# Feed-forward gate and u in transposed layout, heads loaded four at once, and a new order table, in a sparse-attention and gated-MLP kernel

## The chip, the cores and the metric

The kernel runs on one core of a Trainium2 chip. The metric is the device time of one execution in microseconds (us), the median of several. Traces are from the hardware profiler. Engines are named as in the profile: PE (TensorE matmul), PEld (its weight loads), DVE (VectorE), ACT (ScalarE), POOL (GpSimd), SP (SyncE, which here only issues DMAs).

## What is computed

For 4 batches of 8 heads, 768 positions and head size 64: every query attends to the 6 best of the 24 key chunks of 32 positions, chosen by an upper bound from each chunk's minimum and maximum of k; then a gated feed-forward (spatial gating unit) runs on the joined heads.

```python
# attention, per batch and head (q, k, v: 768 x 64)
k_min, k_max = min and max of k over each chunk of 32
ub  = sum(maximum(q * k_min, q * k_max))        # 768 x 24, causal
top = the 6 largest chunks of each row
attn = softmax(q k^T / 8 where chunk in top and causal)
x   = attn v                                     # heads joined: 768 x 512 per batch
# feed-forward, per batch
h = relu(x @ w_in); u, v = h[:, :512], h[:, 512:]
v_n = (v - mean) / sqrt(var + 1e-6)
v_s = w_spatial @ v_n + b_spatial[:, None]       # mixes positions
out = (u * v_s) @ w_out
```

## The kernel before

**Work units.** Heads are worked in 16 pairs (two heads that are neighbours). A head's 768 positions are 6 tiles of 128. Each pair goes through `load_ops`, `prep_ops` (`prep_first` for the first) and `attend_ops`; after every fourth pair a batch is complete and `mlp_ops` runs for it.

**Loading.** `load_ops` issues, on POOL's queue, one DMA for k of both heads (`kp`), two for q (`qs`, one for each head) and one for v (`vt`); the DMA also casts f32 to f16. For the first pair a head's k or q may instead go through SP into an f32 tile `stage` and be cast by an engine.

**Preparing a pair.** k is transposed into `kT`, either by PE (6 matmuls with the identity, then a copy out of PSUM on DVE or ACT) or by a transposing DMA on SP's queue. The chunk extremes are six DVE instructions: two of `t1` (16 against 16), two of `t2` (8 against 8), two reductions into `kmm` (lines L477, L480, L483); for the first pair one head at a time (L580, L584, L588). Small copies spread them into `km` and copy `kT` into `kh` (helper lines L243 for ACT, L245 for POOL, L249 for DVE). q is transposed by PE (L505), evacuated as `rq`, multiplied with `km` (the bounds, L517), and `max8` and `select` write the chunk choice into `qs`, which is transposed into `a` (PE, L553, or SP's DMA).

**Attention.** Scores come out on PE in six groups of columns for each head (L672), ACT makes the exponentials `e` out of PSUM (L683), the causal triangle is put on either by an extra PE matmul (L675), POOL (L694) or DVE (L692), and 21 matmuls of 65 columns multiply with v (L703). DVE normalises into `x16` (L713, L717), which PE (L734) or a DMA (L727) transposes into `xT`.

**Feed-forward of a batch.** For each of 6 position tiles: `v` = 4 matmuls of 512 columns (L752), relu into `vraw`, statistics (L758, L760), and DVE's `vn` (L769). `u` = 4 matmuls of 512 columns with `xT` as weights (L779), relu into `u`. The spatial product: 6 matmuls of 512 columns with `wsT` as weights (L793); then one DVE instruction makes `g = (product + bias column) * u` (L797). `g` has positions on partitions, so it is transposed into `gT`: on SP's queue (L801) or by PE (L807) with a copy. The output product is 4 matmuls of 512 columns (L814), a copy `o`, and a store from SP's queue (L819).

**The order.** Nothing of the order on an engine is left to a scheduler. Every operation is first entered in a list with the engines that could do it and their costs. The string `PLAN` is then run through: each three characters are one operation, the first two its number (in base 64) and the third its engine and PSUM bank. Operations that have two forms (PE or DMA for a transpose, PE or POOL/DVE for the triangle) stand in the list twice, and the table names one of them. So each engine's queue, SP's and POOL's among them, is the table's order, and an instruction that waits holds up all that stand behind it on its engine.

```python
for c in range(0, len(plan), 3):
    hi, lo, how = (DIGITS.index(x) for x in plan[c:c + 3])
    o = self.ops[64 * hi + lo]
    ...
    if o.take is not None:
        o.take.tile = self.banks[how // 4 - 1]
    if len(o.alts) > 1:
        o.emit(list(o.alts)[how % 4])
```

Of the kernel before, what the change touches and what calls it, by code (L numbers as in the profile page):

```python
# [8 lines left out]
F32 = mybir.dt.float32  # L9
F16 = mybir.dt.float16  # L10
# [4 lines left out]
P = 128  # L15
# [22 lines left out]
def blocks(half):  # L38
# [13 lines left out]
    "0k00000140F00900500600K00O00V00l10Q00J00q00X00280R10U00C00wC0N00A003G0m00G00800T10r10M00W01FK0B0"  # L52
    "2N00s00H00I007016O0S13h02RS0x00z00y00/00+01311511102P01001411G01H02O01Q11I01J01711K01L03i004W121"
    "1M04/02S01O10P01R43j01N11802U00v01981S01A02V02e21P11B01T12W00YG1C01UC1V02h25002f23lK2g21DW0Z02X0"
    "0D03m12Y05101W02Z01E12iS1X02k053O2j01Y42d23p00f01r82a22c21Z03r01oG2b22lK2Q05413z18L02m040C2DW1lS"
    "3+124O1t05703o08N02748M00e01q04112n01y83q01n02901/G2o03t01+03s02102AS2sK5K43w05603v12C02q81iG3u0"
    "2t05804202602F05L03US3W01k03RK3x05M03GO5900g03y143C1aW9f04402r04503T03/10E01c01dS4603J423G3X83L0"
    "1f039K9h03Z05A02H02I02xW8P45B02z033S3B05I15E25C08Q05D23I05F24AC3O85J14B048W1hK1v08g49g03Q08S05NC"
    "4901w08i05G13508h14iO4k05204CW5O02J03k05P01x00a04E05H14a84c02K04QS8U02u42w05Q04FG8T03NO4H03b03c0"
    "8V03d08W0Az04NW4oK4d84P06PC3049jG8X08b036W6Q05UO8Z08Y08a04f04l83205S45V04KCCH09k00L04q00c03804TK"  # L60
    "4n08e15T08f16JO9m04V09n04rW6K04t04M09+G5u88jK5Z42/W3D08k05xC5WOA008c14S05b08l05w09/05kS0d05Y04J4"
    "5z04X05m063866O60G9o04Y08m06505eC9y18d15g04Z03E08qS9w16204hK6988o46B09p09q09r08r04v03F08p09u25nC"
    "5hGB189t00b09v2B206809s05p04w04x0B505j05/S3fWA+09TOA/0FR09Q49R0A1C3g15d8A209U06D08tG4z49x1A30CI0"
    "5r05s0A4092K8u077W4+09z18/O930900CLG98C6LK6R49NO6E0990A50Gl05t06F09i0CM06M19F89WCCJ06HS6fKB709G0"
    "6VGB406I09X0B90BF2B609I8B80CO06pC0h0BH29J06W0CP0BE1BIS7809O06X0BK1BA0790BG0BB06q06S0958BJ07GOCQ0"
    "8wG6T4CR06g06Y0BC0CT0FVSBD0BLW8x06aG6U1Ca19Y1FS06r0BM0FW09607H07I06b0B006c0BN08O06z46h0AkCAl0CS0"
    "CX0Aq87DS6Z0FT0AMOCZ1AN09A06+0BO06/0AZGAa06s0CcKAEW6i0CY16d06j0CV06uCAF0FZ0CU0CW16e06v06w09K0AhO"
    "An46k0Cd0BP0Ce06l0AJG6t0Ar00i0Ao07AW700I30AK07MC7N07O06x0Ai0CfK6N8Cb1Cg0710AS46O06y07206n0Ch08y0"
    "7E06m0Ci07JGFY0ABCAs0AP87F0AcOAd07K0Fk1AQ07B07309LS9Z0740Gr08zOFm8Cj0Ae07C0AT0Gn06o07L09B0JN0AC0"
    "C8K750Fl17ZW9C0760BV4BdGAU0Fj17a07jCC90BW0Be0Fi1BgKBh0Af47b0I90Fa0Fb0Fc0At0BmG9a0AG0Fd0BYKFf07k0"  # L70
    "9b07l0Fn19D0C2SAu0Bn0Fo1Fe2BjOBtG7P8Fg0Fh07c07m0Bu0FpW7Q0C30C5CGm0Av0Gs0B/4I50Fq0Bk0C60BZ0BwGBx0"
    "81S820C00DPOI40JP07R0DMCDSKDT0Gt0DQ0Fr0Fs0DEWFt0Bo0Gv0AHGAV0Cs47S0IA0H017U8CK0AW0AX0Gu07d0DN0By0"
    "DJK7V0DK0DU0IC0CA0Ba0Ct0IE08309c0Nr0Aw08BOD4GD50H4C7o87p0Gw0H61IB0ID0Go0840C+KCp4Cq08C0IF0DBGC/0"
    "DC0DF0DG07t88D0Bb47u0D1KD20Gx0G+2Bp0CxSCy0BzGG/2Gz1H11IJ0D60CB0Bq0GOWH50H21Br07v0CC0G8KG90CD0GWC"
    "Gy1GP08E0FzS7W47w0DHGH32DV0Cu0CE0F+0G5KDW0DX0GLWJROH78GX0JS0CvSIH0GTCJO0D70H80GZG7X0JV0GM0GU0II0"
    "H90G60Gc4Jh17Y0Gd0IOOIG1G0WHA07gCIP1DbKIQ07q4IR8MX0G10D80D90JX07h0DZOIS0JZ0Ga0HB0GBWGESDgCGe1GC0"
    "Da0JU0FU0MZ0IT0GF0E3G850Jf1NvWJe2Jg1Dc08F0IL17r0Dh0DlODm0E40IU0JW0Dd1De0IK2Di0Dn0JY0Do0Dj0Dk0D+S"
    "D/0E01Dv4GG0ED8Nw1P90IV0E10Jc0Jb2HtCE50HVKHW0HSOHqWEE0Hu0EF1IM1Jd2HYGJa0HZ0E20Hr0EJS7x0JiKHHCHI0"
    "Dw0Nz0N/0Dp0Df0Dx0GQ0Ny0Jk0Jj1EGGHf8IN1Dq0EH0HwWN+0EI0E60Dy0Dr0E70GRCGf0ES4Du0HT0Md0EPKEQ0Ns0ER1"
    "JQ0ET0Hg0EK0Hx0Gg0EU1Dz0E80G207i0JlGJm0MY0EL0HnOJ08J10G3KGH0HKWDs0884HL0Jn0Jo0EMSGI0Ho0E90Dt0Iz8"  # L80
    "HiWHj0EA0Jp0Gh0Hk0I60Me0Mg0EN0Mf0IbGEB0EO0HPOHQ0Mh0EC07s0Nt0GJ0Ic07+W7/0EpSJ5CEq0Ha1Mj0Mo1IjOHy0"
    "J8G890EVWEW0Mp1EX08I4J90I+0IpGMsKIe8Mi0Er0Ik0Mk0Mm1Gi0Mr2HlOIq0EY0Mn2O10EZ0J60If0Mq1Ml0QU0KHWEfG"
    "Eg0Mt0PDCEs0O00HM0Is8PE0Mu1Eh0JBS8J0PB0MvKIt0Ez4PA0O30JC0Hz0JECIg0O52Ei0Mw0HN8Hb0JF0Mx0KKGMy0E+0"
    "KYSKI0KL0ImCOAKO41E/0H+0H/0Ej0KZ0FHWFI0QT0OB0PG0FJ0Mz0Hc0QV0OC1F00JvGIn0Iu1PI0O20F7SPH0KVOO71O82"
    "Jw0Hd0KSKODCOE0KT0O91K74PJ0800K80JG0F80F90KW0KAGEt0FK0KP88K0FA0O61IhKOF0KQ0KM0PU4QZ0J20PS1K4WJ3O"
    "Ka0JH0JI0KB0JySPW1K50K18KNGJz0J+0K20OG0JJ0KC0Kb0PL0Iv0EmCNfWIw0NZONHSKc0Ec8Ix0NUKNg0NI0N3WJ/SPK0"
    "PV0KD08A0Kd0NE4PO1KE0KF0QoGPN2Ed1Qq0Na0I00NV0N6OEwKN40NiWNF0PM0En1NcSN70Ex0Qp0Kf4PP0NKOPX8LVKNj0"
    "Kg1L4WKrCNd0NRGQb0JK0PT2PY0PZ0NB4KmSKs0Kn0NS0Qd0L50LW0N80OH0Pa0Qa0Qc0Qe0Qf0ONGP08NL0Kt0NC0F10OYO"
    "Ma0OeCKo0L94Nu0Qj1Ku0LA0P10LX1Nk0Pb0Of0KhSOQ8L60Ki0Kv0Qg0OzCLSKLPWLQ0Kj1OZ0LB1Qh0ObOQl0OR0Qi2PQ1"
    "Kk0OO0Oc0OV8O+0OtSLR1QrGNW0Kp0Qs0Kq0LT0NX4Nl0OS0N9OEe0Ou0LYCOwWOW0FL0Q3SLU0LZ0Ox0PR1Ph8Nm0Pi0Qm1"  # L90
    "Qt0Qu0Nn0NM0NN0Qk1Q40PyKK/WQ6GQ70FB0LC0Kl0La1Eo0Kw0QE8QF0L00Kx0L11L20L30F44F50Pz0OoSOp0PpGP21OlC"
    "Pq0QB8QC0Om0NO0L70L80LD0NP0FOWQH4Q81LMKQI0LJSPC0LE0PvGKy0Kz0QW0LN0LO1LK0Qv0QK8QL0Og0LF0PkOLL0Pl0"
    "Ey0FECOT4Q/8Oh0LlKLG0Oq0OrSLH0P30LI0FP0Oi0Pw0K+0Oj0Pm0R00RGOLvWRH0LbGMN8P40P50PsOLm0Lc0Pt0R74QM1"
    "R80Ln0Ld0FF0P+0Lo0Lw0Q9SLe0Qn1RbORQ4RVKRW0Rc0RR0QN0RNCPnGP/0MDKRO0RDOQO0QP0P60No0R2SME0R30Lf0Re4"
    "Q00R41RACQ10Lp0Lx0RE0QQ0RS0RYSMO0RB0Ly0Rf0MP0RI0MF0SYORTGRZ0R5CF60RJ0Rg0Rh0FQ0RK0M34RL0Ri0Rj0MG0"
    "M40M50RnWRlSMQ0M60RxCRsGS5KRm1Rt0Ry0SP8Rz0R+0Ru1Rv0R/0SASRw0SF4Ro0SG0SH0SI0Rp0Rq0S60SQ0SB0M70Lz0"
    "MH0S70SJ0LsCRr0SC0S00S80S10MR0LiGSV4S30S90SD0SW0Lj0SSWS40ST0MAKSZ0FG0SE0M0SS20SK0SL0SM0Sa1SX0S/G"
    "SR0SN0SO0SU1T94Lk0M11Lt0Lu0TA0MB0T00MC0Sh8Si0Sj0M20T10Sk0T20SrOSs0St0Sl0MKCTB0Su0TJKTK0SwWML0TC0"
    "T30MUSMM0Sb8SoGSc0T6OSx1MV1TD0Sd1SyCSp0TT4TL0SeWSz1Sf0TU0TV0TM0MW0TOSTGGSq0T70Sg1TW0TP1T80TH0TY8"
    "TQOS+0TR0TI0TS0TZ0TaCTb0Tc0"  # L100
# [95 lines left out]
def kernel(  # L196
# [35 lines left out]
    G_XBAR = 3  # L232
# [41 lines left out]
    bcol = cp.tile([P, NQT], F32, name="bcol")  # L274
    braw = cp.tile([NQT, P], F32, name="braw")
    idf = cp.tile([NQT, NQT], F32, name="idf")
# [4 lines left out]
    ws_raw = cp.tile([P, NQT, S], F16, name="ws_raw")  # L281

    kp_r = ring(3, [P, 2, NQT, D], F16, "kp")
    qs_r = ring(4, [P, NQT, 2, P], F16, "qs")
    v_r = ring(4, [P, 2, NQT, D + 2], F16, "vt")
    stage_r = ring(4, [P, NQT, D], F32, "stage")
    kT_r = ring(2, [P, S], F16, "kT")
    kh_r = ring(3, [P, 2, S], F16, "kh")
    t1_r = ring(2, [P, 2, NCH, CHUNK // 2], F16, "t1")
    t2_r = ring(2, [P, 2, NCH, CHUNK // 4], F16, "t2")  # L290
    kmm_r = ring(2, [P, 2, NCH], F16, "kmm")
# [14 lines left out]
    u_r = ring(12, [P, DH], F16, "u")  # L306
    g_r = ring(4, [P, DH], F16, "g")
    gT_r = ring(6, [P, KO, P], F16, "gT")
# [21 lines left out]
    def const_ops():  # L330
# [23 lines left out]
        for j in range(len(qs_r)):  # L354
            s.op(("DVE", 0.4, 0.45), lambda j=j: preset(qs_r[j]), -98 + j,
                 w=[("sel", j)])
            s.op(("DVE", 0.1, 0.2), lambda j=j: nc.vector.memset(v_r[j][:, :, :, D:D + 2], 1.0), -97 + j,
                 w=[("ones", j)])
# [6 lines left out]
        for j in range(len(kh_r)):  # L365
            for hi in range(2):
                s.op([("ACT", 0.72, 0.87), ("DVE", 0.45, 0.58)], lambda e, j=j, hi=hi: copy(
                    e, kh_r[j][D * hi:D * hi + D, hi, :], ex, False), -40 + 10 * j, r=["ex"], w=[("exrow", j, hi)])
        s.op(("SP", 0.45, 0), lambda: nc.sync.dma_start(out=braw, in_=moe_b_spatial.rearrange("(t p) -> t p", p=P)),
             -60, w=["braw"], load=0.1, tag="lb")  # L370
        s.op(("DVE", 0.06, 0.16), lambda: nc.vector.tensor_copy(idf, identity[0:NQT, 0:NQT]), 19, r=["identity"], w=["idf"])
        bb = Bank("tr")
        s.op(("PE", 0.25, 0.47), lambda: nc.tensor.transpose(bb.f32[:, 0:NQT], braw, idf), 20, r=["braw", "idf"], w=[bb], take=bb)
        s.op([("DVE", 0.07, 0.2), ("ACT", 0.1, 0.25)], lambda e: copy(e, bcol, bb.f32[:, 0:NQT]), 20, r=[bb], w=["bcol"], drop=bb)

    def both(qs):
        return qs.rearrange("p t h c -> p t (h c)")[:, :, D:D + P].rearrange("p t (h c) -> p t h c", h=2)

    self_n, staged = [0], [[] for _ in stage_r]
    PAIRB = P * 2 * NQT * D * 2 / 120e3  # L380

    def load_ops(i, key):
        b, hp = divmod(i, HP)

# [492 lines left out]
```

## Time and profile before

| | |
|---|---|
| median of 3 runs | 195.15 us (194.39 to 195.46) |
| profiled execution, its own time | 195.44 us |
| span of the program in it | 193.7 us |
| PE busy | 184.4 us (95%), 2079 matmuls |
| DVE busy | 160.8 us (83%) |
| ACT busy | 150.0 us (77%) |
| POOL busy | 115.2 us (59%) |
| q0 (DMAs issued by POOL) | 12.00 MB, 85.9% of 16 engines' span |
| q1 (DMAs issued by SP) | 16.26 MB, 46.2% |

The profiled execution is 0.29 us over the median and has 1.7 us outside its span. Busy times of PE come from modelled ends of pipelined matmuls; the start of one matmul and the start of the next tell more. A group's line in the profile reads: line, engine, operation, written tile <- read tiles, shapes, count | busy time, mean length of one | idle time just before them, and what ended most of it.

### The profile page before, as it was taken

The page shows a single profiled execution, that of the slowest core. Times are in us where ns is not written, and L with a number is a line of the kernel's source. Part 1 is how long each engine was busy: PE and PEld are TensorE (multiplying, and loading weights), DVE is VectorE, ACT ScalarE, POOL GpSimd, SP SyncE. Part 2 cuts the span into 40 slices and gives each one's busy share as a digit, 9 for nine tenths or more (in the row PEclk, how much of TensorE's full clock was granted, in tenths as well). Part 3 has the DMA queues.
Part 4 walks back from the last instruction along what each step waited for, and adds up shares of the span by engine and source line. Part 5 has one row for each costly group of instructions (what it writes and reads, how often), then busy time and mean ns, then how long its engine had stood idle before and what let it go on. Part 6 is the DMA issues. An engine that isn't in the chain of part 4 may idle for free.

```text
span 193.7 us, 5676 instructions
## 1 busy us (share of the span) xinstructions
PE 184.4 (95%) x2079; PEld 123.7 (64%) x2079; DVE 160.8 (83%) x575; ACT 150.0 (77%) x326; POOL 115.2 (59%) x198
## 2 busy tenths in 40 slices
PE   7589999799999999999999999999999999999992
PEld 7477989686667667765665668655756664444450
DVE  7989998788999999989999799796998446995460
ACT  7999999799999888888979879697987742651232
POOL 7999999599899999587709984264811230000000
PEclk9969999999999999999999999999999999999999
DMA  7999999999999999999999999999990582534634
GB/s 107 142 153 151 188 158 111 174 153 155 168 151 140 198 140 150 147 140 159 173 189 181 134 127 291 165 106 192 98 153 30 108 141 65 115 131 137 181 144 162
DMA packets 119495, 28.61 MB, mean 148 GB/s; under 512 B 114086, under 2 KB 116396, under 8 KB 119468
## 3 DMA queue, kind: packets, MB, share of 16 engines
q0 software_dynamic: 75648, 12.00, 85.9%
q1 hardware_dynamic: 43820, 16.26, 46.2%
q8 instruction: 16, 0.26, 0.6%
q14 instruction: 11, 0.09, 0.2%
HBM read 24.38 MB, written 6.29 MB: 158 GB/s over the span
## 4 chain that ended last, share of the span: by engine, by line
PE 69%; DVE 11%; DMA 6%; ACT 6%; POOL 4%; issue 2%; ACTq 0%; DVEq 0%; POOLq 0%
PE bank L793 16%; PE bank L672 12%; PE bank L814 11%; PE bank L703 8%; PE bank L779 8%; PE bank L752 8%; DMA vt<-in_v_dram 4%; ACT e L683 2%; DMA kp<-in_k_dram 2%; DVE vn L769 2%; DVE st L758 2%; PE bank L505 2%; POOL kh L245 1%; ACT kh L243 1%; DVE m L533 1%
## 5 line engine op out<-in xcount | busy, mean ns | idle before, releaser
L683 ACT ACTIVATE e<-bank 128x512 f16<-128x512 f32 (+2 forms) x192 | 92.9, 556 | 14.1 <-PE bank L672 11.7
L672 PE MATMUL bank<-a,kh 128*128 128x128 f16 (+2 forms) x384 | 57.3, 259 | 0.4 <-ACT e L683 0.4
L672 PEld LDWEIGHTS <-kh 128*128 128x128 f16 x384 | 32.1, 98 | 15.5 <-issue 0.5
L694 POOL TENSOR_SCALAR_AFFINE_SELECT e<-e 128x384 f16<-128x384 f16 x40 | 21.6, 546 | 29.1 <-ACT e L683 28.1
L793 PE MATMUL bank<-vn,wsT 128*128 128x512 f16 x144 | 37.1, 379 | 0.1
L703 PE MATMUL bank<-vt,e 128*128 128x65 f16 x672 | 27.5, 193 | 1.0 <-DMA vt<-in_v_dram 1.0
L703 PEld LDWEIGHTS <-e 128*128 128x128 f16 x672 | 25.1, 97 | 4.4 <-DMA vt<-in_v_dram 1.1
L245 POOL COPY kh<-kT 64x384 f16<-64x384 f16 x46 | 23.5, 512 | 6.1 <-PE bank L672 4.0
L398 POOL DMA_DIRECT2D qs<-in_q_dram x31 | 26.0, 844 | 0.3 <-issue 0.3
L779 PE MATMUL bank<-w_in,xT 128*128 128x512 f16 x96 | 25.9, 379 | 0.0
L752 PE MATMUL bank<-w_in,xT 128*128 128x512 f16 x96 | 24.2, 379 | 0.0
L814 PE MATMUL bank<-w_out,gT 128*128 128x512 f16 x96 | 24.1, 379 | 0.0
L797 DVE SCALAR_TENSOR_TENSOR g<-bank,bcol,u 128x512 f16<-128x512 f32 x24 | 17.2, 742 | 4.2 <-PE bank L793 2.7
L793 PEld LDWEIGHTS <-wsT 128*128 128x128 f16 x144 | 12.8, 98 | 10.4 <-issue 0.2
L243 ACT COPY o<-bank 128x512 f32<-128x512 f32 x19 | 11.0, 594 | 10.2 <-PE bank L814 9.2
L717 DVE TENSOR_TENSOR x<-bank,rec 128x384 f16<-128x384 f32 x32 | 17.4, 549 | 0.4
L758 DVE BATCH_NORM_STATS2 st<-vraw 128x6 f32<-128x512 f32 x24 | 15.9, 681 | 2.1 <-ACT vraw L253 1.8
L398 POOL DMA_DIRECT2D vt<-in_v_dram x16 | 16.5, 1032 | 0.0
L398 POOL DMA_DIRECT2D kp<-in_k_dram x16 | 16.4, 1026 | 0.0
L769 DVE TENSOR_SCALAR vn<-vraw,mv,rs 128x512 f16<-128x512 f32 x24 | 14.5, 627 | 0.6 <-ACT rs L765 0.6
L814 PEld LDWEIGHTS <-gT 128*128 128x128 f16 x96 | 9.0, 98 | 8.7
L752 PEld LDWEIGHTS <-xT 128*128 128x128 f16 x96 | 8.9, 98 | 8.3
(99 smaller groups left out, 284.7 us busy)
## 6 DMA issues: line engine op xcount, KB each, us to landing
out_dram<-o SPq DMA_DIRECT2D x24, 256.0 KB, 2.4
vt<-in_v_dram POOLq DMA_DIRECT2D x16, 192.0 KB, 6.4
qs<-in_q_dram POOLq DMA_DIRECT2D x31, 96.0 KB, 4.5
kp<-in_k_dram POOLq DMA_DIRECT2D x15, 192.0 KB, 6.2
ws_raw<-in_moe_w_spatial_dram POOLq DMA_DIRECT2D x3, 384.0 KB, 8.2
w_in<-in_moe_w_in_dram POOLq DMA_DIRECT2D x4, 256.0 KB, 7.8
w_out<-in_moe_w_out_dram POOLq DMA_DIRECT2D x2, 256.0 KB, 6.0
gT<-g SPq DMA_TRANSPOSE x19, 2.7
```

Source lines behind the costliest of these rows:

```text
L245: nc.gpsimd.tensor_copy(o, f)
L398: s.op(("POOL", cost, 0), lambda: nc.gpsimd.dma_start(out=o[0] if len(o) == 1 else o[2], in_=f[0] if len(f) == 1 else f[2]), key, w=w, loa ...
L672: mm(bs.f32[:, col:col + n], lhsT=kh[:, hi, t * P:(t + 1) * P], rhs=a[:, f // P:(f + n) // P, hi, :], start=True, stop=not on)
L683: s.op(("ACT", *act_cost(n)), lambda g=g, n=n, bs=bs, e=e: nc.scalar.activation(out=e[:, BASES[g]:BASES[g] + n], in_=bs.f32[:, 0:n], func= ...
L694: nc.gpsimd.affine_select(out=o, in_=o, compare_op=Alu.is_ge, fill=0.0, base=0, channel_multiplier=-1, pattern=[[0, 3], [1, P]])
L703: mm(o[:, qi, :], lhsT=e[:, c:c + P], rhs=vt[:, hi, t, 0:D + 1], start=first and n == 0, stop=last and n == len(bl) - 1)
L752: mm(bk.f32, lhsT=x[:, ko, t * P:(t + 1) * P], rhs=w_in_sb[:, ko, DH:DFF], start=(ko == 0), stop=(ko == NDO - 1))
L758: s.op(("DVE", 0.60, 0.74), lambda vraw=vraw, st=st: nc.vector.bn_stats(st, vraw), kk, r=[("vr", nvr[t])], w=[("st", nst)])
L769: s.op(("DVE", 0.46, 0.6), lambda tt=tt, j=j, mv=mv, rs=rs: nc.vector.tensor_scalar(vn[:, tt, :], in0=vr_r[nvr[tt]], scalar1=mv[:, j, 0:1] ...
L779: mm(bk.f32, lhsT=x[:, ko, t * P:(t + 1) * P], rhs=w_in_sb[:, ko, 0:DH], start=(ko == 0), stop=(ko == NDO - 1))
L793: mm(bk.f32, lhsT=wsT[:, si, t * P:(t + 1) * P], rhs=vn[:, si, :], start=(si == 0), stop=(si == NQT - 1))
L814: mm(bo.f32, lhsT=gT[:, db, :], rhs=w_out_sb[:, db, :], start=(db == 0), stop=(db == KO - 1))
```

## The change

**u and the gate are made transposed.** `u` now has `w_in` as weights and `xT` as the moving operand: 8 products of 384 columns (4 matmuls each), with features on partitions. The spatial product has `vn` as weights and `wsT` as the moving operand: again 8 products of 384 columns (6 matmuls each). The result stands in the layout that the output product needs as weights, so `g`, its 19 DMA transposes (L801) and its 5 on PE (L807) are gone. The bias runs along columns now: a tile `bias` of 128 x 768, loaded by one SP DMA with stride 0 over partitions, is added by DVE into an f32 tile `tmp`, and a second instruction, on POOL or DVE, multiplies `tmp` with `uT` into `gT`. An output tile of 128 positions needs all four feature blocks of its half of the positions. `vn` may be done by ACT too, with a small DVE instruction `nb` (two a batch) for its bias.

**Pairs are two apart and loaded four heads at once.** Pair `i` holds heads `x` and `2 + x` of a group of four. Two heads' k lie behind each other as they are loaded, one DMA loads k of four heads, two DMAs q of two heads each, one v of four; for the first group k and q come head by head, and two of them may go through SP. `w_in`'s rows are permuted to match and loaded in 4 DMAs of full rows.

**Extremes of two pairs at once.** k of four heads is transposed in one go (one DMA, or 12 PE matmuls and two copies), and the six DVE instructions of the extremes run on four heads, one time for two pairs.

**A new table.** All orders and engine choices are new. Read from the two tables (counts where they differ most):

| operation | before | after |
|---|---|---|
| PE matmuls for u / spatial product | 96 / 144 of 512 columns | 128 / 192 of 384 columns |
| PE transposes of g / k / x (128 columns) | 20 / 72 / 36 | 0 / 36 / 24 |
| PE triangle matmuls | 48 | 42 |
| SP transposes of a / x / k / g | 11 / 10 / 4 / 19 | 11 / 12 / 5 (twice the size) / 0 |
| DVE `g`, 512 columns, PSUM | 24 | 0 |
| DVE bias add, 384 columns, PSUM | 0 | 32 |
| gate multiply, 384 columns: POOL / DVE | 0 | 23 / 9 |
| DVE extremes, 1 / 2 / 4 heads | 12 / 90 / 0 | 24 / 0 / 42 |
| `vn`: DVE / ACT | 24 / 0 | 11 / 13 |
| relu of u: ACT / DVE | 13 / 11 of 512 | 22 / 10 of 384 |
| POOL loads of k, q, v | 63 | 35 |
| `kh` and `km` copies on POOL / ACT / DVE | 79 / 38 / 11 | 95 / 21 / 12 |

```diff
-    kp_r = ring(3, [P, 2, NQT, D], F16, "kp")
-    qs_r = ring(4, [P, NQT, 2, P], F16, "qs")
-    v_r = ring(4, [P, 2, NQT, D + 2], F16, "vt")
+    kp_r = ring(2, [P, 4, NQT, D], F16, "kp")
+    qs_r = ring(3, [P, 2, NQT, 2, P], F16, "qs")
+    v_r = ring(3, [P, 4, NQT, D + 2], F16, "vt")
...
+        if n:
+            load("k", k, 0, 4, key, False)
+            load("q", q, 0, 2, key + 0.1, False)
+            load("q", q, 2, 2, key + 0.15, False)
         else:
+            for j, h0 in enumerate((0, 2, 1, 3)):
+                load("k", k, h0, 1, key + 0.2 * j + 2 * (j > 1), j < 2)
+                load("q", q, h0, 1, key + 0.1 + 0.2 * j + 2 * (j > 1), j < 2)
+        load("v", v, 0, 4, key + 0.2, False)
...
+    def chunk_ops(n, heads, key):
...
+        for m, op in ((0, Alu.max), (1, Alu.min)):
+            s.op(("DVE", c1, c1 + 0.12), lambda m=m, op=op: nc.vector.tensor_tensor(
+                t1[:, m, hs], in0=kc[:, :, :, 0:16], in1=kc[:, :, :, 16:32], op=op), key, r=kt, w=wk("t1", m))
...
+                    if e == "ACT":
+                        nc.scalar.activation(vn[:, tt, :], vr_r[nvr[tt]], func=Act.Identity, bias=nb[:, j, :], scale=rs[:, j, :])
...
+        for j in range(2 * KO):
+            hf, db = divmod(j, KO)
+            c = slice(N * hf, N * (hf + 1))
...
+                        mm(bk.f32[:, 0:N], lhsT=w_in_sb[:, ko, db * P:(db + 1) * P], rhs=x[:, ko, c],
+                           start=(ko == 0), stop=(ko == NDO - 1))
...
+                        mm(bk.f32[:, 0:N], lhsT=vn[:, si, db * P:(db + 1) * P], rhs=wsT[:, si, c],
+                           start=(si == 0), stop=(si == NQT - 1))
...
+            s.op(("DVE", 0.48, 0.61), lambda bk=bk, tmp=tmp, c=c: nc.vector.tensor_tensor(
+                tmp, in0=bk.f32[:, 0:N], in1=bias[:, c], op=Alu.add), kk, r=[bk, "bias"], w=[("tmp", ntmp)], drop=bk)
+            def gate(e, tmp=tmp, db=db, c=c):
+                eng = nc.gpsimd if e == "POOL" else nc.vector
+                eng.tensor_tensor(gT[:, db, c], in0=tmp, in1=uT[:, db, c], op=Alu.mult)
...
-                        mm(bk.f32, lhsT=wsT[:, si, t * P:(t + 1) * P], rhs=vn[:, si, :],
-                           start=(si == 0), stop=(si == NQT - 1))
...
-                out=g, in0=bk.f32, scalar=bcol[:, t:t + 1], in1=u_r[nu[t]], op0=Alu.add, op1=Alu.mult),
...
-            s.op(("SP", 1.25, 0), lambda g=g, gT=gT: nc.sync.dma_start_transpose(out=gT, in_=g), kk,
```

## The prediction

> **What bounds the kernel now.** First the page's second part and the chain of work that ended last:
>
> ```profile
> PE   7589999799999999999999999999999999999992
> PE 69%; DVE 11%; DMA 6%; ACT 6%; POOL 4%; issue 2%; ACTq 0%; DVEq 0%; POOLq 0%
> ```
>
> Matmul busy time is modelled, so the row of nines alone proves nothing; the chain says that PE's work is what ended last over 69% of the span, and in its pieces by time all the longer ones after 63 us are PE's, up to the last copy. Next the busy times by stage (columns: stretch, its length, busy us of PE, PEld, DVE, ACT, POOL, granted clock, DMA share, GB/s):
>
> ```profile
> 0.00:20.00 20.00, 15.82 (x206) 13.94 (x207) 18.15 (x93) 18.23 (x39) 18.81 (x31) 0.91 1.76 139
> 20.00:40.00 20.00, 18.75 (x347) 16.89 (x344) 17.46 (x79) 18.43 (x45) 17.37 (x32) 1.00 1.79 159
> 40.00:80.00 40.00, 39.83 (x482) 27.26 (x480) 38.10 (x138) 36.84 (x82) 37.06 (x65) 1.00 1.82 155
> 80.00:120.00 40.00, 40.00 (x458) 26.00 (x455) 36.65 (x138) 34.59 (x75) 27.13 (x46) 1.00 1.52 170
> 120.00:160.00 40.00, 40.00 (x456) 25.66 (x453) 30.24 (x94) 30.26 (x68) 14.80 (x27) 1.00 0.96 130
> 160.00:193.70 33.70, 30.06 (x153) 13.98 (x151) 20.15 (x39) 11.68 (x23) 0.00 (x0) 1.00 0.43 132
> ```
>
> The first 40 us are short of PE work everywhere; DVE stays nearly full to 120 us, and after 160 us only PE is. Then the timeline of PE, for how densely matmuls follow each other:
>
> ```profile
> 96.14 2.32 PE L779 MATMUL bank<-w_in,xT 128*128 128x512 f16 x10
> 98.30 0.41 PE L517 MATMUL bank<-km,rq 128*128 128x48 f16 x10
> 98.88 0.82 PE L703 MATMUL bank<-vt,e 128*128 128x65 f16 x21
> ```
>
> Ten matmuls of 512 columns take 2.16 us from start to next start: 216 ns each. Over all records the median interval from a matmul's start to the next is 216 ns (512 columns), 162 (384), 109 (256), 56 (128), 32 (65), 25 (48). Adding these intervals gives 177.0 us of the 188.6 us between the first start and the last; 11.6 us are gaps, of which 9.8 lie in the first 40 us and only 1.8 in the other 150. With 1.05 us ahead and 4.0 behind (last matmul, a 0.59 us copy, the store) that is the span of 193.7 us. So from 40 us on the kernel is PE's issue, and a matmul taken out is worth its interval.
>
> **PE's sum.** Gone are 20 transposes of `g`, 36 of k and 12 of x (the table sends more of x and k through SP's DMA) and 6 triangle matmuls: 74 x 56 ns = 4.1 us. u and the spatial product keep their columns: 240 x 216 ns = 51.8 us against 320 x 162 ns = 51.8 us, so 80 more instructions cost 0 to 0.2 us. Everything else on PE has the same count. Net -4.1 us. All of it lies on the path after 40 us, if no other engine is late then; that has to be shown by stage.
>
> **The other engines.** Rows used (mean ns of one before the idle time):
>
> ```profile
> L797 DVE SCALAR_TENSOR_TENSOR g<-bank,bcol,u 128x512 f16<-128x512 f32 x24 | 17.2, 742 | 4.2 <-PE bank L793 2.7 <-issue 1.1
> L717 DVE TENSOR_TENSOR x<-bank,rec 128x384 f16<-128x384 f32 x32 | 17.4, 549 | 0.4
> L477 DVE TENSOR_TENSOR t<-kT 128x384 f16<-128x384 f16 x30 | 10.9, 371 | 0.0
> L483 DVE TENSOR_REDUCE kmm<-t 128x24 f16<-128x192 f16 x30 | 9.7, 340 | 0.2
> L398 POOL DMA_DIRECT2D vt<-in_v_dram x16 | 16.5, 1032 | 0.0
> L694 POOL TENSOR_SCALAR_AFFINE_SELECT e<-e 128x384 f16<-128x384 f16 x40 | 21.6, 546 | 29.1 <-ACT e L683 28.1
> ```
>
> DVE. Out go 24 `g` (17.8 us), 30 x (371 + 302 + 340) of extremes (30.4), 13 `vn` at 627 (8.2), 6 `kT` and 3 `gT` copies (4.5). In come 32 bias adds; the nearest row is L717, also 384 columns from PSUM with two inputs, 549 ns: 17.6 us (up to 742 each by L797: 23.7). Extremes of four heads are extended from one head's (255, 205, 244) and two heads' rows, whose difference is the price of the columns: 603 + 496 + 532 ns, 14 times, 22.8 us, and four more single heads, 2.8. Nine gates at 549: 4.9. Eight `nb` as L713's 187: 1.5. Smaller shifts (u's relus -2.0, `rq` +2.4, `o` +2.1 and the rest) add 3. Net -8 us, at worst -2.
>
> ACT. 13 `vn` at 598 (the relu `vraw`, same shape) +7.8, u's relus +3.3, against 17 `kh`/`km` copies -5.0, `rq` -3.5, `o` -1.8, `gT` -1.2: even. `vn` uses a function ACT has not run here; the trace has one table load of 1.28 us in all, which Exp, Ln, Relu and Copy share. The cost lies between no load and two for each `vn` (26 x 1.28 = 33 us of ACT); I take none. The Trainium skill (ScalarE: Activation LUTs, "Table sets: the hidden batching unit") says that identity is in every set, which no row here can show; by it no load is added.
>
> POOL. 63 loads (26.0 + 32.9 = 58.9 us) become 35: six of one head at 844, 14 of two at 1026, 15 of four at an extended 1390, together 40.4. `kh` and `km` copies add 4. The 23 gates are the unknown: no POOL instruction of before reads two tensors. L694, one input over the same 384 columns, takes 546 ns; reading two in turn would be 1.09 us. The ends are 0.55 and 1.09 and, where it has to wait for DVE, half a microsecond more; I take 1.0, since two inputs must be read: 23 us. POOL ends up 9 us higher, at some 124 of 190.
>
> The Trainium skill (GPSIMD Engine Reference, "Engine selection") speaks against this: two-input elementwise work is about twice as slow there as on VectorE; its 2.6 cycles per element would make a gate 0.83 us plus dispatch, an estimate, and 23 gates 19 us.
>
> By stage, cumulated over the tables' orders with the same rows (durations overlap a little, so DVE counts some 10% high): between the 72nd and the 168th exponential PE's work is 77 us before and 70.5 after, DVE's 77 and 66.5, POOL's 51.5 and 50, ACT's 73 and 70. DVE gains the margin that it lacked. A POOL gate waits for DVE's add, and that for PE; behind it in POOL's queue stand the next pair's `kh` copies and triangles, for which scores and the v product wait. 13 of the 23 gates lie in that stretch. With 20 us of POOL's time left there, each could be 2.5 us before POOL sets the pace: cost nothing.
>
> SP's queue loses 19 transposes, gains one of k and two of x; in order it stands ahead of output stores, which nothing waits for but `o`. The DMA landing of `gT` (2.7 us) leaves the path and add plus gate (0.55 + 1.0 us) takes its place.
>
> **The end.** The table puts two output tiles (2 x 0.86 us) between the last spatial product and the first output that needs it; add, then gate on DVE (0.55 + 0.55), beside a gate on POOL for the product before, lie under these 1.7 us with 0.2 to 0.4 us to spare. Cost 0, or 0.5 if a POOL gate takes 1.5.
>
> **The start.** Landings in the trace come at 0.63 us a head (k at 7.23, q 7.91, two heads' k 9.16, q 9.79, 10.42, 11.10). In the new order PE's first score stands behind the transposes of k of heads 4 to 7 and q of the second pair. q's last issue comes after some 7 us of POOL's queue (five single loads, one of four, three small fills), lands 4.5 us later, about 12; transposes (1.0) and a copy (0.8) make a first score at 13.3 to 14.1, against 14.06 in the timeline of before. PE has 6.35 us of work ahead of it, before 6.2. The first v has 24 head loads up to its end instead of 16: 15.35 + 8 x 0.63 = 20.4 us; its first use was at 20.63 and has 1.1 us more PE work ahead, 21.7. So no gain and no loss, to within 2 us either way; the clock, 0.91 in the first 20 us, can move it by 1.
>
> Forecast: 195.44 - 4.1 = 191.3 us for a run like the profiled one, which stands 0.29 over the median; 191.0 us.
>
> **Rivals.**
> - *A quicker start.* ACT, 18.2 of 20 us busy at the start, gives 17 copies to POOL. If the 9.8 us of gaps fall by 3: 188. Against it: DMA landings, not ACT, stand ahead of the first score.
> - *DVE and POOL hold each other up.* The instructions of tile `vn`, shortest, median and longest in ns, and with them `t` (324, 348, 666):
>
> ```profile
> L769 DVE TENSOR_SCALAR vn<-vraw,mv,rs x24: 499/544/1116, 58.4 to 173.2; 128x512 f16<-128x512 f32 x24
> ```
>
>   Something costs such a DVE instruction up to 0.6 us. The Trainium skill (SBUF — State Buffer, "Who interferes with whom") has a port pair that the two lock for a whole instruction. If each of 13 gates costs DVE 0.6 us, that is 8 us, and DVE (66.5 + 8) passes PE's 70.5: 4 us come back, 195.
> - *The first v of four heads is late* (slower). One DMA now must land four heads before the first v product, and behind that product PE's whole queue waits. At the pace of the v that landed at 35.10, 3.1 us after the one before it (1.56 us a head), it lands at 15.35 + 8 x 1.56 = 27.8, a wait of 6.1 us that nothing later returns: 197.1. It decides from 1.3 us a head on. Against it: 0.63 in all landings before 13 us.
> - *The change doesn't do what it says*: u and product pay more than 162 ns for each 384-column matmul. At 180 ns it is 320 x 18 = 5.8 us, 196.8. The 96 score matmuls of that width show 162, so I give it nothing of its own.
>
> **How the numbers follow.** Forecast 0.70 (its own range 189.2 to 193.0: the start's 2 us), quicker start 0.07, hold-up 0.14, late v 0.09. A difference of 0.5%, about 1 us, is what a measurement of this kernel can tell. Faster: 0.70 + 0.07 + 0.05 of the hold-up = 0.82; same: 0.06 of the hold-up + 0.02 of the late v = 0.08; slower 0.10. The range leaves out half of the quick starts and most of the slower case: 188.6 to 195.8.
>
> **What would show it.** Right: no L801 or L807 rows; 320 matmuls of 384 columns with 162 ns intervals; PE's intervals sum to about 173 us and gaps after 40 us stay under 3 us; DVE busy near 153 us; first score near 14 us. Wrong: PE gaps between 60 and 130 us ended by DVE's add or POOL's gate; adds over 700 ns or gates over 1.5 us; a v product idle for microseconds near 21 us on DMA `vt`; a start later than 16 us.

## The result, and the profile after

The changed kernel takes 213.75 us (median of 4 runs, 210.56 to 217.2) against 195.31 us for the kernel before on the same chip: a ratio of 1.087, 95% interval 1.069 to 1.105. Forecast were 191.0 us. The profiled execution took 213.25 us with a span of 211.5. All ratios leave out executions at a disturbed clock, so a ratio can be lower than the two medians beside it (e5_order below); by its ratio the change costs 16.9 us.

The same parts of the page as before, the PE row, the row of the granted clock and the chain:

```profile
PE   7568999079999399999988999999999999999992
PEclk9958999859999859999996999999999999999999
PE 54%; DMA 25%; POOL 11%; DVE 4%; issue 2%; ACT 2%; POOLq 0%; ACTq 0%
```

The row of the clock before:

```profile
PEclk9969999999999999999999999999999999999999
```

PE has holes at about 38, 70 and 110 us, the clock drops in or right behind each, and DMA's share of the chain went from 6% to 25%. By stage (columns as in the prediction):

```profile
0.00:20.00 20.00, 14.22 (x159) 12.51 (x159) 16.79 (x90) 16.42 (x31) 17.98 (x32) 0.83 2.04 149
20.00:40.00 20.00, 16.38 (x295) 14.96 (x295) 16.01 (x66) 17.51 (x39) 17.84 (x33) 1.00 1.64 156
40.00:80.00 40.00, 32.45 (x385) 24.28 (x386) 26.84 (x99) 25.77 (x54) 23.95 (x40) 0.83 1.63 132
80.00:120.00 40.00, 37.52 (x412) 25.24 (x410) 34.03 (x116) 32.69 (x72) 30.22 (x55) 0.96 1.72 156
```

From 40 to 80 us PE, which was full there before, has 32 of 40 us and a clock of 0.83, and every other engine is less busy as well, so no other engine's work is what holds PE up. The waits of PE (us in all, times, longest) name the transfers; the one for v before, then the two largest after:

```profile
PE bank L703 <- DMA vt<-in_v_dram: 1.0, 1, 1.0
```

```profile
PE bank L704 <- DMA vt<-in_v_dram: 9.3, 2, 7.3
PE bank L540 <- DMA qs<-in_q_dram: 3.5, 1, 3.5
```

Summed as in the prediction, PE's intervals are 173.06 us (before 177.02), 3.96 less, and the gaps 33.2 us (before 11.6). That is the whole difference: +21.6 - 4.0 = 17.6 of the span's 17.8. The gaps by stretch of 40 us from the start: 18.1, 8.9, 5.2 and 0.7 us, before 9.8, 0.9, 0.4 and 0.5. A gap is not only the wait. From the last part of the wait from 36.29 to 43.84 us (v) on the trace has half clock for 6.8 us, likewise with 69.47 to 73.26 (q) again 6.8, after 109.67 to 112.02 (v) 3.4, and at the start 6.8 instead of 3.4: 23.9 us in all, where the kernel before has 3.4. In a part of that time PE still waits; the matmuls that it issues there lie 7.7 us in sum over their usual intervals, and 1.4 us before. The Trainium skill (TensorE: Matmul & The Clock Gate, "Why this matters for your kernels") wants no idle gap of PE over some 3 us; here one of 2.35 us was enough, while one of 3.30 us in a later run (e11, at 99.7 us) was followed by none, so these traces give no fixed threshold.

Where the transfers are late, first the DMA issues of before, then of after (KB each, median us from issue to landing):

```profile
vt<-in_v_dram POOLq DMA_DIRECT2D x16, 192.0 KB, 6.4
w_in<-in_moe_w_in_dram POOLq DMA_DIRECT2D x4, 256.0 KB, 7.8
w_out<-in_moe_w_out_dram POOLq DMA_DIRECT2D x2, 256.0 KB, 6.0
```

```profile
vt<-in_v_dram POOLq DMA_DIRECT2D x8, 384.0 KB, 9.9
w_in<-in_moe_w_in_dram POOLq DMA_DIRECT2D x4, 256.0 KB, 14.9
w_out<-in_moe_w_out_dram POOLq DMA_DIRECT2D x2, 256.0 KB, 11.8
```

The first w_in load landed at 38.89 us, 8.7 us after the q ahead of it on POOL's queue (30.22); k (41.30) and the v that PE waited for (43.79) stood behind it. The page's DMA row is at nine tenths in nearly all slices up to some 140 us in both kernels, so there is little room to catch up in when a load is late.

### The profile page after: what moved, and what is told of

Same layout as the page of the kernel before. It is cut to its first block, busy times and chain, and to the rows that moved or that the text cites. A ratio compares the mean times of both kernels' runs of the same rounds, so it can differ in the third digit from the quotient of the medians.

```text
span 211.5 us, 5616 instructions
## 1 busy us (share of the span) xinstructions
PE 188.2 (89%) x2084; PEld 132.3 (63%) x2084; DVE 157.8 (75%) x551; ACT 153.2 (72%) x323; POOL 124.7 (59%) x208
## 3 DMA queue, kind: packets, MB, share of 16 engines
q1 hardware_dynamic: 39856, 15.73, 41.9%
## 4 chain that ended last, share of the span: by engine, by line
PE 54%; DMA 25%; POOL 11%; DVE 4%; issue 2%; ACT 2%; POOLq 0%; ACTq 0%
DMA vt<-in_v_dram 12%; PE bank L810 12%; PE bank L673 9%; PE bank L794 8%; PE bank L704 7%; PE bank L829 7%; PE bank L752 6%; DMA qs<-in_q_dram 5%; POOL qs L406 5%; DMA kp<-in_k_dram 4%; DMA xT<-x 2%; PE bank L540 2%; POOL kp L406 2%; POOL km L244 1%; POOL kh L244 1%
## 5 line engine op out<-in xcount | busy, mean ns | idle before, releaser
L673 PEld LDWEIGHTS <-kh 128*128 128x128 f16 x384 | 32.7, 100 | 12.7 <-issue 1.7
L810 PE MATMUL bank<-wsT,vn 128*128 128x384 f16 x192 | 39.7, 328 | 0.0
L819 POOL TENSOR_TENSOR shared<-tmp,uT 128x384 f16<-128x384 f32 x23 | 22.0, 962 | 21.8 <-DVE tmp L814 21.6
L794 PE MATMUL bank<-xT,w_in 128*128 128x384 f16 x128 | 28.6, 344 | 0.0
L752 PE MATMUL bank<-w_in,xT 128*128 128x512 f16 x96 | 24.4, 379 | 0.1
L814 DVE TENSOR_TENSOR tmp<-bank,bias 128x384 f32<-128x384 f32 x32 | 17.2, 551 | 9.6 <-PE bank L810 9.1
L829 PE MATMUL bank<-w_out,shared 128*128 128x512 f16 x96 | 23.7, 379 | 0.1
L810 PEld LDWEIGHTS <-vn 128*128 128x128 f16 x192 | 17.3, 98 | 9.5
L252 ACT ACTIVATE uT<-bank 128x384 f16<-128x384 f32 x22 | 10.5, 493 | 15.6 <-PE bank L794 15.4
L406 POOL DMA_DIRECT2D qs<-in_q_dram x18 | 17.8, 992 | 0.2 <-issue 0.2
L714 DVE RECIPROCAL rec<-bank 128x6 f32<-128x6 f32 x32 | 6.0, 189 | 14.9 <-PE bank L704 13.7
L794 PEld LDWEIGHTS <-w_in 128*128 128x128 f16 x128 | 11.9, 102 | 6.6 <-issue 0.7
L252 ACT ACTIVATE vraw<-bank 128x512 f32<-128x512 f32 x19 | 11.2, 604 | 5.4 <-PE bank L752 5.2
```

What stands on the lines that cost most here:

```text
L252: nc.scalar.activation(o, f, func=Act.Relu, scale=sign)
L406: s.op(("POOL", 0.62 + 0.19 * nh, 0), lambda: nc.gpsimd.dma_start(out=dst(name, h0, nh), in_=src(a, h0, nh)), key, w=w, load=PAIRB * nh / ...
L673: mm(bs.f32[:, col:col + n], lhsT=kh[:, hi, t * P:(t + 1) * P], rhs=a[:, f // P:(f + n) // P, hi, :], start=True, stop=not on)
L752: mm(bk.f32, lhsT=x[:, ko, t * P:(t + 1) * P], rhs=w_in_sb[:, ko, DH:DFF], start=(ko == 0), stop=(ko == NDO - 1))
L794: mm(bk.f32[:, 0:N], lhsT=w_in_sb[:, ko, db * P:(db + 1) * P], rhs=x[:, ko, c], start=(ko == 0), stop=(ko == NDO - 1))
L810: mm(bk.f32[:, 0:N], lhsT=vn[:, si, db * P:(db + 1) * P], rhs=wsT[:, si, c], start=(si == 0), stop=(si == NQT - 1))
```

## The experiments

**1. The cut of w_in's load.** The change cuts w_in into 4 DMAs whose source is two blocks of 64 rows. In the trace w_in's packets (512 of 2 KB in all) take 173 ns each in the median, and from 28 to 35 us, while the first of the four DMAs is alone, only 2.2 of them are in flight at a time (later, with more of the four under way, 6 to 8). e1_win16 cuts the same bytes into 64 rows by two, with nothing else changed:

```diff
-            g, x = divmod(o, 2)
-            rows = moe_w_in[4 * D * g:4 * D * (g + 1)].rearrange("(hh x d) f -> x hh d f", hh=2, d=D)[x]
+            g, hh = divmod(o, 2)
+            rows = moe_w_in[4 * D * g + 2 * D * hh:4 * D * g + 2 * D * (hh + 1)].rearrange("(x d) f -> d x f", d=D)
...
-                out=w_in_sb[:, o, :], in_=rows)
+                out=w_in_sb[D * hh:D * (hh + 1), 2 * g:2 * g + 2, :], in_=rows)
```

> The changed kernel, with its four loads of w_in cut otherwise: each writes 64 partitions of two row blocks (outer dimension of the source 64), instead of 128 partitions of one row block whose source has an outer dimension of 2. Same bytes, same number of DMAs, same order. Theory 1 (the w_in loads run on two of the 16 DMA engines and hold up every load queued behind them on those two): the first w_in lands 2 to 3 us after the q ahead of it instead of 8.7, the second v by 37 us instead of 43.8, the PE stall of 7.5 us near 36 us shrinks to under 2 us and the half clock after it goes; 202 to 207 us. Rival (one load of four heads is what makes v late): w_in's cut does not matter, v lands at 42 to 44 us again, 211 to 215 us. Rival 2 (the later stalls at 69 and 110 us have causes of their own): they stay, and the time does not go under 201 us.

Measured: 211.18 us, ratio 1.074 (1.065 to 1.083). The first w_in now lands 1.0 us after the q ahead of it instead of 8.7, and the wait for v shrinks from 7.3 to 3.5 us, but the q wait grows to 4.9 and a second v wait stays:

```profile
PE bank L705 <- DMA vt<-in_v_dram: 6.3, 2, 3.5
PE bank L541 <- DMA qs<-in_q_dram: 4.9, 1, 4.9
```

So the cut does to the loads right behind it what theory 1 says, but not more: v lands at 40.63 us and not by 37, between the two theories, and the time is the rival's; taking the cut out returns 2.5 us by the ratios, within their intervals. Other late transfers stand behind it. The other way round, the kernel before with the change's cut (its rows of w_in stand in another order than x's):

> The kernel before, with w_in loaded by the four DMAs of the change (source outer dimension 2; the rows stand in the order of the change, which does not fit this kernel's heads, so only its time is read). Theory 1: loads of v and k behind it land 6 to 9 us later, PE stalls for 4 to 8 us between 35 and 50 us with a half clock behind it; 200 to 208 us. Rival (four-head loads): two-head loads stay punctual, 194 to 197 us.

204.33 and 209.59 us, too far apart to tell the price. The same kernel once more:

> The kernel before with the change's four loads of w_in (two source blocks of 128 rows each), as e2_before_win2, timed in five rounds: the cut of w_in by itself, against the e1_win16 that takes it out of the changed kernel. As there the rows of w_in stand in another order than x's, so the output is not the reference's. Theory A (each of these loads runs on two DMA engines and holds the queue behind it for some 8 us): 203 to 206, the first load of w_in 12 us or more from issue to landing, the v that the table issues ahead of it still on time, what stands behind it late. Theory B (e2's time was chance): within 1 us of before.

203.84 us, ratio 1.043 (1.039 to 1.047): the change's loads of w_in alone cost the kernel before 8.5 us. Here v was issued ahead of w_in and came in time (34.05 us); w_in landed 8.3 us after it, at 42.38, and k behind it at 43.62, for which PE stood:

```profile
PE bank L467 <- DMA kp<-in_k_dram: 6.5, 2, 5.7
```

This is PE's longest wait there, and the row of the clock on its page drops behind it as in the changed kernel:

```profile
PEclk9969999966999999999999999999999999999999
```

The Trainium skill (DMA: Bandwidth & Descriptors, "Why a DMA increments its semaphore by 16 and not by 1") says that a DMA is spread over the largest number of engines, up to 16, that divides the outermost size of both access patterns. With an outermost size of 2 that is two engines; the 2.2 packets in flight, and the 1.0 us with 64, agree.

Would it do to move the slow load out of the way? e3_win_behind_v is the changed kernel with the first w_in moved behind the second v in the table (in these lists of operations `ld3 k` is the load of k of group 3, counted from 0, `xbar` a transposing DMA, `tr` a transpose on PE and `evac` its copy out of PSUM):

```diff
 POOL's order: ... ld2 q 2-3 | - ld w_in | ld3 k | ld1 v | + ld w_in | ...
```

> The changed kernel, with the first w_in load moved in the table behind the second v of four heads, nothing else. Theory 1: k and v of heads 12 to 15 and 4 to 7 no longer stand behind it and land by 36 us, the 7.5 us stall shrinks to under 2 us; w_in itself now lands at 45 to 50 us, so the first feed-forward products may wait instead; 203 to 212 us. Rival (four-head loads): v lands at 40 us or later, 210 to 215 us.

217.19 us (one run), over both theories. v landed at 36.21 and the wait at 36 us was gone; the w_in loads took 23.1 us from issue to landing (median), PE stood from 43.17 to 52.58 us, again at 53.94 and 58.88 for over 2 us, and had 20.5 us at half clock behind the first wait. The profile names no release for that first wait; in it, three transposes on SP's queue were 15 to 21 us under way. So the lateness is handed on and not removed.

**2. The bias.** A tile of 128 x 768 is filled from 3 KB by a DMA that repeats its source; it is third in SP's queue, at 1.90 us, and writes 393 KB while the first heads are loaded. e4_bias_late is e1_win16 with this operation moved down the table:

```diff
 SP's order: ld0 k0 | ld0 k2 | - ld bias | xbar k3 | + ld bias | xbar x2 | ...
```

> The changed kernel with the cut of w_in's load from e1_win16 (each of its four DMAs over 64 source rows) and with the broadcast load of the bias moved down SP's queue, from third place to behind the first four-head transpose of k. Theory A (the 393 KB that the bias writes at 1.9 us hold up the first loads of k): the first POOL load of k lands at 5.2 to 6 us instead of 9.2, the first score multiplies at 15 to 16 us instead of 18.2, the half-clock stretch at the start is 3.4 us instead of 10.2, and the time falls from 211.2 to 203-207. Theory B (the start is late because k and q of heads 0 and 2 are staged in another order, whatever the bias does): the first load of k still lands after 7 us, the first score after 17 us, and the time is 210 to 212. The stalls near 68 us (q) and 109 us (v) stay under both theories.

208.50 us, ratio 1.060 (1.051 to 1.069), 2.6 us less than e1_win16 by the ratios, whose intervals overlap a little, and between the times of the two theories. The first POOL load of k lands at 5.14 us (e1_win16 9.19). The first score came at 16.69 us (18.2), not at the 15 to 16 of theory A. In the kernel before, with this load added into a tile that nothing reads:

```diff
             nc.sync.dma_start(out=braw, in_=moe_b_spatial.rearrange("(t p) -> t p", p=P))
+            nc.sync.dma_start(out=bias, in_=bass.AP(moe_b_spatial.tensor, moe_b_spatial.offset, [[0, P], [1, S]]))
```

> The kernel before with one DMA added, third in SP's queue: the change's broadcast of the bias, 128 rows of 3,072 bytes, into a tile that nothing reads. It prices that load by itself. Theory A (it holds up the first loads): the first POOL load of k lands at 7 to 9 us instead of 5.2, the first score is 1.5 to 4 us later than at 14.1, and the time is 198 to 202. Theory B (it lies beside the other transfers): first score within 0.5 us of 14.1, time 194.5 to 197.

198.41 us, ratio 1.010 (1.007 to 1.014). The first load of k lands at 8.72 us instead of 5.24, the first score comes at 16.97 instead of 14.06. Theory A holds: 2.0 us by the ratio, for 3 KB of data.

What is left of the late start in e4_bias_late is not a load. PE waits 3.2 us, to 11.98, for the `rq` that ACT makes from 11.22 on; ACT waited for the `rq` that DVE starts at 10.70, behind 19 of the 24 short instructions of the extremes (four heads one by one). In the kernel before DVE's `rq` starts at 8.71, behind only two heads' twelve. The prediction counted these 12 more and put them at 2.8 us, but not ahead of the first bounds.

**3. The order of the loads.** e5_order is e4_bias_late with q of the fifth group ahead of the sixth k, and the fifth v ahead of the seventh q:

```diff
 POOL's order: ld2 v | + ld4 q 2-3 | + ld4 q 0-1 | ld5 k | ... | - ld4 q 2-3 | - ld4 q 0-1 | ...
               ... ld w_out0 | + ld4 v | ... ld6 q 2-3 | ld6 q 0-1 | - ld4 v | ...
```

> As e4_bias_late, and three loads moved in POOL's queue: the two q loads of the fifth group of four heads go ahead of the k load of the sixth (384 KB), and the v load of the fifth group goes ahead of the q loads of the seventh, right behind the first load of w_out. Theory A (the stalls near 68 and 109 us are these transfers waiting behind 384 KB loads in a queue that is full, and each costs its length and a 6.8 us stretch of half clock): both stalls are under 1 us, the half-clock stretches after 60 us are gone, and the time is 8 to 14 us under e4_bias_late. Theory B (the DMA engines are the bound all through that part, so a load moved forward only makes another late): new stalls of the same sum at k or v, and the time is within 3 us of e4_bias_late.

Median 208.56 us, ratio 1.047 (1.039 to 1.055), so about 2.6 us under e4_bias_late by the ratios. The waits for this q and v are gone from the profile, which is of the slowest of the four executions (212.05 us), and in it others stand in their place, above all for `a`, the transposes on SP's queue:

```profile
PE bank L674 <- DMA a<-qs: 6.4, 2, 5.5
PE bank L705 <- DMA vt<-in_v_dram: 3.4, 1, 3.4
```

That is nearer to theory B: while the DMA engines are full, an earlier load makes something else late. How large the new waits are in the quicker executions is not shown.

**4. Transposes on the queue.** Of the 74 transposes and triangles that left PE, 36 are k's, now made by SP's DMAs. e14_before_k_on_dma does this alone in the kernel before, whose other orders stay:

```diff
 pairs 6, 7, 8, 11, 13, 14: - tr k (PE, 6 matmuls) | - evac kT   + xbar k (SP, one DMA)
```

> The kernel before with the 36 transposes of k of the seventh to ninth, twelfth, fourteenth and fifteenth pair taken off TensorE and given to SP's DMA queue, where the change's table has them too. TensorE loses 36 x 56 ns = 2.0 us, and six evictions go. Theory A (the queue is the bound to some 110 us, so transposes moved there cost more than TensorE gains): 196.5 to 201, with waits for kT or for loads behind it between 40 and 100 us. Theory B (these transposes lie beside the loads): 193 to 194.5, the 2 us that the prediction counted.

202.78 us, ratio 1.039 (1.034 to 1.044). PE's intervals fall by 2.04 us as counted, to 174.99, and its gaps rise from 11.6 to 22.4: 8.8, 7.6, 4.2 and 1.4 us by stretches of 40 us. So 2 us on PE are bought for 10.8 us of waiting. How, the waits of DVE and PE show:

```profile
DVE t L477 <- DMA kT<-kp: 8.5, 3, 5.4
PE bank L672 <- DVE qs L539: 2.9, 1, 2.9
```

The transpose issued at 37.31 us landed at 44.16. DVE's extremes stand in the table where a transpose on PE would be done; DVE waits there with all that is queued behind, and PE after it. Neither the kernel before nor the changed one has a wait of DVE for a `kT` that a DMA makes: the changed kernel's table leaves more time there. So this is the price in an order that was not made for it. Nor did SP's queue grow as a whole: its packets took 41.9% of 16 engines' span of 211.5 us, before 46.2% of 193.7. What these transposes cost in the changed kernel has to be seen there.

The opposite step in the changed kernel: four blocks (counted from 0: k of groups 3 and 4, the masked q of pairs 5 and 6; 48 transposes) back from SP to PE, on top of e4_bias_late:

```diff
 k groups 3, 4: - xbar k (SP)   + tr k (PE, 2 x 6 matmuls) | + evac kT (2)
 pairs 5, 6:    - xbar a (SP)   + tr a (PE, 2 x 6 matmuls) | + evac a (2)
```

> e4_bias_late with four blocks of transposes taken from SP's DMA queue and done by TensorE as the first groups' are: k of the fourth and fifth group of four heads, and the masked q of the sixth and seventh pair. TensorE gets 48 more transposes of 128 columns (48 x 56 ns = 2.7 us) and ACT or DVE eight more evictions. Theory A (from 30 to 75 us the DMA engines are the bound, and these transposes, 4 to 13 us from issue to landing, stand in the same queue as the loads): the stalls near 66 us (q) is under 1.5 us, the v stall near 36 us stays at 3 to 4 us because it lies ahead of these transposes, one 6.8 us stretch of half clock goes, and the time is 201 to 205 against 208.5. Theory B (the loads' own bytes are the bound, not the transposes): the stalls stay, TensorE's 2.7 us come on top, 209 to 212.

206.55 us, ratio 1.051 (1.038 to 1.064). The bias load stood behind the transpose that was taken away, so it went back to the start (first score 17.4 us). Once more with the bias issued by POOL, behind the last w_in:

> e7_k_on_pe once more with the bias out of the way: there the load of the bias stood behind the DMA transpose of k that was taken away, and went back to the start. Here it is issued by GpSimd behind the last load of w_in; the same four blocks of transposes are on TensorE. Theory A (the transposes in the shared queue made the later loads late): first score at 16.5 to 17 us as in e4_bias_late, no q stall near 66 us, and 202 to 205. Theory B (what e7 gained was chance): 207 to 210.

207.01 us, ratio 1.056 (1.049 to 1.063). In both, the q wait near 66 us is gone, as theory A has it; the gaps from 40 to 80 us fall from 7.7 to 4.7 us (e10), from 80 to 120 from 5.7 to 3.5. But PE's 2.6 us of transposes eat half of that: by the ratios the two take 205.6 and 206.4 us, each between its two theories, and the gain over e4_bias_late is within the intervals. The waits went as theory A has it, the time did not follow. The v wait near 36 us (3.6 us in e10) is untouched, as expected.

**5. The whole table anew.** With the DMA times of these traces, a search over order and engines was run on the change's operations and, as a control, on those of the kernel before.

> e4_bias_late with its whole table sorted anew: a local search over the order of the operations and their engines, with each DMA's time on a shared queue as the traces of before and after show it (four heads of k or v 3.5 us, two heads of q 1.6, a transpose of four heads of k 2.2, of a pair's q 1.9, w_in 1.3), and with the transposes of the fourth to sixth k group, of the sixth to ninth masked q and of one x on TensorE. What is computed and each operation's form are the change's. Theory A (the change's operations are no slower; the loss is loads that come late in the order that its table gives): no stall over 1.5 us after 20 us, half clock at the start only, and 188 to 194. Theory B (the four-head loads make the start or the middle slower in any order): stalls of 2 us or more stay between 15 and 110 us, and 197 to 206.

> The kernel before with its table sorted anew by the same search and the same DMA times, with two masked q more on TensorE: the control for e8_after_sorted, for a new order may help any kernel. Theory A (the table of before was already near what its operations allow): 192 to 196. Theory B (the search gains as much here): 186 to 191, and the change is then to be judged against this and not against 195.

e8: 203.78 us, ratio 1.042 (1.034 to 1.050), theory B's time, but with no wait over 1.9 us after 20 us; PE's intervals had grown by 5 us to 178.0, and the bias had gone back to the start of SP's queue (first score 17.2 us). e9: 216.73 us (210.06 to 219.8), worse than either theory; in the execution of 210.06 us PE waits five times, 7.8 us in all, for `a` on SP's queue. So this search is worth nothing as a judge of the best order, and the control says nothing on the change. Two more tables, with later starts, dearer DMA transposes and the bias on POOL:

> The change's operations in a table sorted anew as in e8_after_sorted, with the bias issued by GpSimd (in e8 it stood at the start again), later starts of the engines, dearer DMA transposes (2.6 us for four heads of k, 2.2 for a pair's q) and only k of the fourth to sixth group and q of the sixth to eighth pair moved to TensorE. Theory A (what e8 lost beside its 5 us of transposes was the bias at the start and late loads): first score at 15 to 16 us, stalls under 1.5 us after 20 us, 194 to 199. Theory B (the start of the change is longer in any order): first score after 16.5 us, 200 to 204.

> As e11_sorted_again from another start of the search, with one more masked q and one x on TensorE (1 us of TensorE more, 3 us less on the queue). Theory A (the queue is still the bound in e11): 1 to 3 us under e11. Theory B (the queue has slack by then): 0 to 2 us over e11.

e11: 206.91 us, ratio 1.054 (1.047 to 1.061); e12: 202.50 us, ratio 1.035 (1.031 to 1.039), 3.7 us under e11 by the ratios, more than theory A there says, and the best that was found with the change's operations. e11 missed both its theories: its start was short (first score 15.18 us), but PE waited 3.2 us for q at 47 us and 3.3 us at 100. In e12 the blocks of k groups 3 to 5, of the masked q of pairs 5 to 8 and one more x are on PE, and SP's queue issues nothing from 20 to 80 us. Its stages:

```profile
0.00:20.00 20.00, 14.02 (x175) 12.35 (x176) 16.55 (x88) 15.98 (x31) 17.35 (x27) 0.91 1.99 133
20.00:40.00 20.00, 18.62 (x320) 16.21 (x318) 18.53 (x83) 18.59 (x42) 17.69 (x33) 1.00 1.38 126
40.00:80.00 40.00, 39.77 (x542) 30.53 (x540) 36.19 (x127) 36.95 (x79) 32.86 (x57) 1.00 1.47 126
80.00:120.00 40.00, 38.48 (x455) 26.77 (x454) 35.87 (x121) 35.24 (x82) 27.59 (x43) 1.00 1.23 140
```

PE is full again from 40 to 80 us (39.77 of 40) and the clock is whole, with the same four-head loads; order and transposes changed together, so it is not shown which of the two did it. But its intervals sum to 178.0 us, 1.0 more than before the change: the gain is handed back. The rest of its loss lies in gaps (16.9 us against 11.6), 12.7 of them in the first 40 us. No version that beats the kernel before was found.

## Why the prediction was wrong

The step that failed is the condition that the prediction set on PE's 4.1 us: they lie on the path "if no other engine is late then; that has to be shown by stage". It was shown for PE, DVE, POOL and ACT. The transfers got no term in it: the start was held against the landings of before, and for the rest stands the one sentence "SP's queue loses 19 transposes, gains one of k and two of x; in order it stands ahead of output stores, which nothing waits for but `o`." So late loads outside the start were put at nothing, and PE's gaps after 40 us at under 3 us. The runs show 15.1 us of gaps there and 18.1 for 9.8 before that: PE waits 9.3 us for v and 3.5 for q, and behind these waits it runs at half clock.

Two DMAs that the change adds or reshapes were not priced at all: w_in's new cut costs 8.5 us in the kernel before (e13), the bias 2.0 (e6). Taken out of the changed kernel one after the other they return 2.5 and 2.6 us; that other late transfers hide the rest is likely, but not shown. The sentence on SP's queue counted DMAs (of k five for four, but each of twice the size): the 36 transposes of k that left PE are on that queue, from 41 us on, on the DMA engines that also carry every load, where the 19 of `g` were issued from 72 us on. In the order of the kernel before such a move costs 7.6 us net (e14), by a wait of DVE that the changed kernel does not have; in the changed kernel the q wait near 66 us goes with four blocks of transposes (e7, e10), for a gain within the intervals. The three prices add up to 18.1 us beside the 16.9 measured, but that is chance, for they do not hold in the changed kernel. With w_in and the bias mended it is still 6.0% slower (e4), and how much of that is the order of the loads, the transposes or the four-head loads stays open.

Point by point:

- **PE's sum** was right: -3.96 us for -4.1, and 416 intervals of 384 columns at 162 ns. (The sum of 177.0 does not come from the intervals as listed: with 32 ns for 65 columns it is some 2 us higher in both kernels, and the gaps as much lower. The differences stay.) The rival of 180 ns is out.
- **The other engines** were near in size. From the groups of after (mean ns before the bar's idle time):

```profile
L819 POOL TENSOR_TENSOR shared<-tmp,uT 128x384 f16<-128x384 f32 x23 | 22.0, 962 | 21.8 <-DVE tmp L814 21.6
L814 DVE TENSOR_TENSOR tmp<-bank,bias 128x384 f32<-128x384 f32 x32 | 17.2, 551 | 9.6 <-PE bank L810 9.1 <-ACT e L684 0.3
L774 ACT ACTIVATE vn<-vraw,nb,rs 128x512 f16<-128x512 f32 x13 | 10.1, 814 | 0.0
```

  The gate on POOL is 0.96 us for 1.0, the add 551 ns for 549. `vn` on ACT is 814 ns for 598: that term was 2.8 us short, on an engine with room, and no table load came with it. DVE has 157.8 us, 3 less than before where 8 less were forecast; POOL 124.7 (124). Four heads' extremes took 691, 474 and 541 ns for 603, 496 and 532.
- **"A POOL gate waits for DVE's add"**: PE's waits list no gate, and an add with 0.2 us; the hold-up rival is out as a price. Single DVE instructions do get long (the first step of four heads' extremes 1.74 us at most, 0.69 in the mean), but PE does not stand for them.
- **"The end"** held: gaps of 0.3 us after 160 us.
- **The start** ("no gain and no loss, to within 2 us either way"): the first score came 2.9 us later than before, at 16.99 us. The step took landings at 0.63 us a head from the trace of before and did not ask what the bias, issued at 1.90 us, does to them; and it did not put the 12 more single-head extremes ahead of the first bounds.
- **"The first v of four heads is late"** named a v product behind a four-head load as the slow case, but at the wrong place and for the wrong reason. The first v landed at 22.05 us, near the 20.4 of the forecast, and PE had no wait for it. The second v was late, by 7.3 us in one wait. The cut of w_in ahead of it made about half of that; 3.5 us are left in e1_win16, and what the four heads themselves do is in these, together with the 256 KB of w_in and 384 KB of k that still stand ahead of that v.
- **A stall's price** was taken as its length (6.1 us in the rival of the late v). It is more: in and behind the three long waits, 13.7 us together, lie 17 us at half clock, in which the matmuls issued lose another 5.9 us.

Open: what the four-head loads cost by themselves. No run has them in finer pieces with the rest of the change kept. Whether a good table with the change's operations could reach the kernel before is open too; e12 is 3.5% away.

## What to carry to other kernels

An operation that leaves the bound engine for a queue is moved, not removed: price it on that queue, at the place in time where it goes, and where something waits for it, as the time from issue to landing there (7 us for one transpose in e14) and not as its share of the bandwidth. Of every DMA that a change adds or reshapes, look at the outermost size of its patterns and at the bytes it writes; in the kernel before, a changed cut of 1 MB and a broadcast of 3 KB cost 8.5 and 2.0 us. A row of nines for DMA under a full PE is a reason to give the transfers a term by stage, as the engines have: here 4 us less on PE came with 21.6 us more of gaps.

## What the runs showed of the hardware

- A DMA whose source has two outer blocks moved 256 KB with 2.2 packets in flight, and landed 8.3 to 8.7 us after the load ahead of it on POOL's queue; cut into 64 rows the same bytes landed 1.0 us after it.
- Half clock came after a PE wait as short as 2.35 us, in pieces of 3.4 us; behind a wait of 3.8 us it lasted 6.8. Behind one of 3.30 us (e11) there was none.
- GpSimd multiplied two 128 x 384 tiles (f32 and f16) in 0.96 us where VectorE took 0.66 (medians 0.91 and 0.55); the VectorE add out of PSUM kept its 0.55.
- ScalarE's scaled and biased copy of 128 x 512, f32 to f16, took 814 ns, its relu of the same shape 604.
